# Value products in blocks of four key tiles from the first head on, and half of the later query projections ahead of the attention

## The chip, the cores and the metric

The kernel runs on one core of a Trainium2 chip. The metric is the device time of one execution in microseconds; for several executions the median is given.

## The reference

Two branches share the input `x` (2048 x 512, float32) and are mixed by a gate per row: multi-query attention with 32 heads of 16 columns and one key and one value head, and a gated feed-forward layer with 1792 hidden columns.

```python
q = (x @ wq).reshape(B, S, H, Dh).transpose(0, 2, 1, 3)      # S = 2048, H = 32, Dh = 16
k, v = x @ wk, x @ wv                                        # one head, shared by all 32
p = softmax(einsum("bhqd,bkd->bhqk", q, k) * Dh ** -0.5)
a = einsum("bhqk,bkd->bhqd", p, v).transpose(0, 2, 1, 3).reshape(B, S, H * Dh) @ wo
b = (silu(x @ w_gate) * (x @ w_up)) @ w_down
g = sigmoid((x * gate_w).sum(-1, keepdims=True))
out = g * a + (1 - g) * b
```

## The kernel before

**Arithmetic.** Every projection is done in three matmuls, since each operand is split into a high and a low part of a reduced float32 format: high by high, high by low, low by high (`three`). A job of the class `Job` is one 128 x 512 result in a PSUM buffer "pf" (there are three), made of 12 or 15 such matmuls, its *steps*. When its last step is issued, its `end` empties the buffer.

**Stages.** First `x` is transposed in four chunks of 512 columns, and keys and values are projected. Then come the queries. The query weights are cut into four column groups `m` of eight heads each; `query(m, c)` is the job for group `m` and chunk `c`. Group 0 (the first eight heads) is done at once. The other groups' twelve jobs stand at the head of the list `JOBS`, followed by the feed-forward jobs: gate and up per hidden tile, and down. `fill(GAP)` runs the first 36 steps of the list, three query jobs, as whole 128-row matmuls before the attention begins.

**The attention.** A unit `u` is one head and one of its 16 key tiles. `score(u, j)` makes two matmuls on the two 64-row halves of the array, into one of two PSUM buffers "pss" (1024 columns); `exps` lets ACT write the exponentials into a tile "pt". `mix(u)` multiplies a whole "pt" with the value tile, in four matmuls of 32 columns, and adds into "po". Between scores, `feed(k)` issues `k` steps of jobs: in the attention a job's steps are halved by rows, and `Halves` pairs the low half of one job with the high half of another (each feed issues at most two 64-row matmuls). What order all this has is written out by hand under a manual schedule.

For the first two heads a loop of `BEGIN = 16` rounds does two key tiles each: four scores and eight feeds, then two `mix`. From unit 32 on, `block(k, ...)` does four key tiles: 8 scores and 16 feeds in the order of `STEPS`, then four `mix`. In a block some scores are read half by ACT and half by DVE (letter H in `KINDS`: DVE copies 512 columns out of PSUM and ACT does their exponential later). The first block of all, k = 8, has an order of its own (`TURN`), because it must score ten tiles ahead where others score eight. "pt" comes from the pools `bp` and, from the release of the query pool on, a second pool of the same size.

**Where queries go.** The end of a query job, `keep`, makes three parts: `qh` and `ql`, and `qb`, the absolute value times the largest key norm, of which a running maximum `top` decides at the end whether a safe path must be run. Group 0 uses two passes of ACT and three tiles of the rings "hh" and "hl", seven tiles each; other groups use four passes of DVE, one tile of each ring and one of "hs" or "ht" (two each). DVE's maximum comes last. The three parts go to `q_d` in DRAM by three DMAs (`store`) from the queue of SP, which issues in order; heads of later groups are read back by `load_head`. Stores of group 0 are collected in `STORES` and issued before the last group's weights are loaded. A ring hands a tile out again only when all that read it is done, DMAs included.

**After the attention.** Jobs that are left run as whole matmuls, while the last head's sums are inverted and stored; then `finish` multiplies the attention's output with `wo`, and adds the feed-forward part.

## Time and profile before

| | |
|---|---|
| median of 3 runs | 1343.92 us (1343.49 to 1346.85) |
| the profiled execution | 1344.01 us, its span 1341.9 us |
| busy: PE, ACT, DVE, POOL | 1328.0, 1061.6, 722.4, 391.0 us |
| DMA | 107.79 MB, mean 80 GB/s |
| first score, first value product | 47.93 us, 53.37 us from the span's start |
| first block of four, its value product | 137.35 us |
| last value product ends, output projection begins | 1262.7 us, 1290.2 us |

The busy time of PE counts pipelined matmuls, whose ends are modelled. In rows of the timeline the columns are the start and the length in us, engine, line, operation, what is written and read, the shape and the number; a bracket gives the idle time ahead of it and what ended it. SPq rows are DMA issues on the queue of SP.

### The profile page before, as it was taken

The page shows a single profiled execution, that of the slowest core. Times are in us where ns is not written, and L with a number is a line of the kernel's source. Part 1 is how long each engine was busy: PE and PEld are TensorE (multiplying, and loading weights), DVE is VectorE, ACT ScalarE, POOL GpSimd, SP SyncE. Part 2 cuts the span into 40 slices and gives each one's busy share as a digit, 9 for nine tenths or more (in the row PEclk, how much of TensorE's full clock was granted, in tenths as well). Part 3 has the DMA queues.
Part 4 walks back from the last instruction along what each step waited for, and adds up shares of the span by engine and source line. Part 5 has one row for each costly group of instructions (what it writes and reads, how often), then busy time and mean ns, then how long its engine had stood idle before and what let it go on. Part 6 is the DMA issues. An engine that isn't in the chain of part 4 may idle for free. (4 is left out here: it accounts for less than half of the span.)

```text
span 1341.9 us, 26802 instructions
## 1 busy us (share of the span) xinstructions
PE 1328.0 (99%) x10743; PEld 770.4 (57%) x10743; DVE 722.4 (54%) x1221; ACT 1061.6 (79%) x1463; POOL 391.0 (29%) x408
## 2 busy tenths in 40 slices
PE   9999999999999999999999999999999999999997
PEld 7655555555555555555555555555555555555576
DVE  5554565555455555555464555455454565465432
ACT  4578888888888888888888888888888888888400
POOL 6140321152042151152131241142131241333343
PEclk9999999999999999999999999999999999999999
DMA  8455221131122221141131221231121221222154
GB/s 277 142 173 190 65 60 38 35 107 44 44 86 77 78 80 38 35 107 44 52 122 39 82 79 39 57 83 45 52 61 30 81 79 39 74 68 60 44 161 143
DMA packets 101489, 107.79 MB, mean 80 GB/s; under 512 B 9968, under 2 KB 69616, under 8 KB 99696
## 3 DMA queue, kind: packets, MB, share of 16 engines
q1 hardware_dynamic: 99632, 105.81, 27.5%
q8 instruction: 88, 1.44, 0.5%
q10 hardware_dynamic: 1728, 0.20, 0.1%
q14 instruction: 41, 0.34, 0.1%
HBM read 76.09 MB, written 29.36 MB: 79 GB/s over the span
## 5 line engine op out<-in xcount | busy, mean ns | idle before, releaser
L668 ACT ACTIVATE pt<-pss 128x1024 f32<-128x1024 f32 (+1 forms) x1024 | 842.0, 876 | 177.3 <-PE pss L660 146.3
L664 DVE COPY pt<-pss 128x512 f32<-128x512 f32 x354 | 244.8, 692 | 415.6 <-PE pss L660 380.6
L680 PE MATMUL po<-pt,vaug 128*32 128x512 f32 x4096 | 467.6, 595 | 0.0
L660 PE MATMUL pss<-qs,ks 64*128 64x512 f32 x2048 | 403.1, 417 | 1.1 <-ACT pt L668 1.1
L660 PEld LDWEIGHTS pss<-qs,ks 64*128 64x128 f32 x2048 | 193.7, 184 | 218.4 <-ACT pt L668 183.6
L680 PEld LDWEIGHTS po<-pt,vaug 128*32 128x32 f32 x4096 | 119.2, 109 | 260.2 <-issue 255.2
L668 ACT ACTIVATE pt<-pt 128x512 f32<-128x512 f32 x354 | 195.7, 620 | 0.0
L176 PE MATMUL pf<-xh,wgl 64*128 64x512 f32 (+1 forms) x440 | 162.0, 392 | 0.0
L176 PE MATMUL pf<-xh,wgh 64*128 64x512 f32 (+1 forms) x440 | 160.5, 391 | 0.5 <-DVE acc L331 0.2
L176 PE MATMUL pf<-xl,wgh 64*128 64x512 f32 (+1 forms) x440 | 160.2, 390 | 0.0
L176 PE MATMUL pf<-xh,wuh 64*128 64x512 f32 (+1 forms) x440 | 158.4, 391 | 0.7 <-DVE sign L403 0.3
L176 PE MATMUL pf<-xl,wuh 64*128 64x512 f32 (+1 forms) x440 | 158.2, 390 | 0.0
L176 PE MATMUL pf<-xh,wul 64*128 64x512 f32 (+1 forms) x440 | 157.3, 391 | 0.0
L106 POOL CAST wgh<-wraw 128x512 fp32r<-128x512 f32 x56 | 36.1, 644 | 402.6 <-PE pf L176 311.8
L176 PE MATMUL pf<-wdh,hh 64*128 64x512 f32 (+1 forms) x427 | 143.4, 391 | 1.7 <-DVE hh L106 1.7
L176 PE MATMUL pf<-wdh,hl 64*128 64x512 f32 (+1 forms) x427 | 144.1, 390 | 0.0
L176 PE MATMUL pf<-wdl,hh 64*128 64x512 f32 (+1 forms) x427 | 143.4, 390 | 0.0
L689 DVE RECIPROCAL rsb<-rsb 128x128 f32<-128x128 f32 x128 | 117.1, 935 | 10.1 <-issue 8.2
L106 POOL CAST wuh<-wraw 128x512 fp32r<-128x512 f32 x56 | 35.1, 626 | 298.2 <-PE pf L176 245.3
L176 PEld LDWEIGHTS pf<-xh,wgh 64*128 64x128 f32 (+1 forms) x440 | 78.5, 185 | 9.8 <-issue 2.5
L176 PEld LDWEIGHTS pf<-xh,wuh 64*128 64x128 f32 (+1 forms) x440 | 77.3, 185 | 9.3 <-issue 3.7
L176 PEld LDWEIGHTS pf<-xl,wgh 64*128 64x128 f32 (+1 forms) x440 | 78.5, 185 | 6.0
(157 smaller groups left out, 1547.6 us busy)
## 6 DMA issues: line engine op xcount, KB each, us to landing
wraw<-in_B_w_gate_dram SPq DMA_DIRECT2D x56, 256.0 KB
wraw<-in_B_w_up_dram SPq DMA_DIRECT2D x56, 256.0 KB
wraw<-in_B_w_down_dram SPq DMA_DIRECT2D x56, 256.0 KB
qs<-q_d SPq DMA_DIRECT2D x62, 192.0 KB
q_d<-hl SPq DMA_DIRECT2D x18, 256.0 KB
q_d<-hh SPq DMA_DIRECT2D x18, 256.0 KB
o_d<-osb SPq DMA_DIRECT2D x128, 32.0 KB
a_d<-acc SPq DMA_DIRECT2D x4, 1024.0 KB
```

The lines of the kernel that those rows point to most:

```text
L106: eng_hi.tensor_copy(hi, src)
L176: ins = nc.tensor.matmul(self.ps, a, b, start=(i == 0 and not half), stop=(last and half != 0))
L660: nc.tensor.matmul(ps[:, b * CH:(b + 1) * CH], ks[rows, kt * P:(kt + 1) * P], QS[h][rows, j, :], start=True, stop=True)
L664: other = nc.vector.tensor_copy(pt[:, CH:], ps[:, CH:]) if half else None
L668: ins = nc.scalar.activation(pt[:, w], ps[:, w], AF.Exp, scale=SCALE)
L680: nc.tensor.matmul(po[c * 2 * DH:(c + 1) * 2 * DH, :], vaug[:, kt, :], pt[:, c * CH:(c + 1) * CH], start=(kt == 0), stop=(kt == NT - 1))
L689: nc.vector.reciprocal(rsb[:, w], rsb[:, w])
```

## The change

`BEGIN`, `TURN` and their loop go: after an opening of four scores and eight feeds (`OPEN`) all 128 blocks are of four key tiles. For that all six "pt" buffers come from one pool (`PTB = 6`), and its space is had by freeing the query pool ahead of the attention: `qpool` now holds only the chunks 2 and 3 of `x`, and the query weights lie in `wqpool` of their own. The list of query jobs is ordered by chunk (2, 3, then 0, 1) instead of by group, and `GAP` is 72: the six jobs of chunks 2 and 3 run before the attention, as whole matmuls, and are emptied as group 0 is, by ACT with three tiles of the two rings. The six others run in the attention and are emptied by DVE; the scaling, the absolute value with the store, and the maximum are put on the list `DEFER` and run between blocks. `load_wq(3)` is issued before the stores of group 0. The maximum over `top` moves behind the attention.

```diff
-GAP = 36
+GAP = 72
-PTB = 3
+PTB = 6
-BEGIN = 16
-TURN = "SS" + "SFF" * 8
+OPEN = "SFSFFFSFFFSF"
...
+    wqpool = tc.alloc_tile_pool(name="wqpool", bufs=1, side="right")
...
-        WQ[m] = load_split(wq_v[:, :, m * P:(m + 1) * P], f"wq{m}", 1, qpool)
+        WQ[m] = load_split(wq_v[:, :, m * P:(m + 1) * P], f"wq{m}", 1, wqpool)
...
-            if m:
-                qb = wp.tile([P, CH], F32, name="ht" if c % 2 else "hs", bufs=2)
+            behind = m and c in ORDER[:2]
+            if behind:
+                qb = wp.tile([P, CH], F32, name="ht" if (m + c) % 2 else "hs", bufs=2)
                 nc.vector.tensor_copy(qh, ps)
             else:
                 qb = wp.tile([P, CH], F32R, name="hl" if c % 2 else "hh", bufs=7).bitcast(F32)
                 nc.scalar.activation(qh, ps, AF.Copy)
                 nc.scalar.activation(qb.bitcast(F32R), ps, AF.Abs, scale=kmax)
...
+            if behind:
+                DEFER.extend([((m, c), 0.5, scale), ((m, c), 0.7, bound), ((m, c), 0.7, most)])
             else:
-                STORES.append(store)
-            nc.vector.tensor_reduce(top[:, t:t + 1], qb, axis=AX.X, op=ALU.max)
+                if m:
+                    store()
+                else:
+                    STORES.append(store)
+                most()
...
-        jobs = [query(m, c) for m in range(1, KD) for c in range(NCH)]
+        jobs = [query(m, c) for c in ORDER[2:] + ORDER[:2] for m in range(1, KD)]
...
+            load_wq(3)
             run(STORES, NCH)
-            load_wq(3)
             fill(GAP)
+    qpool.release()
...
-            for n in range(BEGIN):
...
-            for k in range(2 * BEGIN // BLOCK, NB):
+            tiles = [(u, j) for u in range(2) for j in range(2)]
+            for what in OPEN:
+                if what == "S":
+                    exps(*score(*tiles.pop(0)))
+                else:
+                    feed(1)
+            for k in range(NB):
                 u = BLOCK * k
-                if k == 2 * BEGIN // BLOCK:
-                    n = u + 6 - (u + 1)
-                    block(k, u + 1, u + 6, TURN, "A" * 2 * n, [f"{i}d" for i in range(2 * n)])
-                elif k == NB - 1:
+                if k == NB - 1:
...
+        nc.vector.tensor_reduce(top[:, KD * NCH:], top[:, :KD * NCH], axis=AX.X, op=ALU.max)
...
-            if len(JOBS) == TC:
+            if len(JOBS) <= TC and OUTS[1] not in OT:
                 load_o(OUTS[1])
```

What this makes of the instructions is seen at three places. The first is PE, in the first head. Before, around the second pair of value products (L660 is a score, L680 a value product, each "pt" one key tile):

```order
L660 MATMUL pss_782<-qs_257,ks_78 128x512 x2
L680 MATMUL po_742<-pt_731,vaug_79 32x512 x4
L680 MATMUL po_742<-pt_751,vaug_79 32x512 x4
L660 MATMUL pss_795<-qs_257,ks_78 128x512 x2
L660 MATMUL pss_799<-qs_257,ks_78 128x512 x2
```

And now, around the first value products (a score is L669, a value product L689):

```order
L669 MATMUL pss_853<-qs_260,ks_78 128x512 x2
L669 MATMUL pss_856<-qs_260,ks_78 128x512 x2
L689 MATMUL po_861<-pt_766,vaug_79 32x512 x4
L689 MATMUL po_861<-pt_780,vaug_79 32x512 x4
L689 MATMUL po_861<-pt_793,vaug_79 32x512 x4
L689 MATMUL po_861<-pt_810,vaug_79 32x512 x4
L669 MATMUL pss_879<-qs_260,ks_78 128x512 x2
```

Where two key tiles stood between scores, four stand.

The second is ACT, where the projections give way to the attention. Before (L217 and L218 empty a query job of group 0, L668 is an exponential):

```order
L217 ACTIVATE hh_501<-pf_488 128x512
L218 ACTIVATE hh_503<-pf_488,kmax_83 128x512
L217 ACTIVATE hh_525<-pf_512 128x512
L218 ACTIVATE hl_527<-pf_512,kmax_83 128x512
L668 ACTIVATE pt_696<-pss_697 128x1024
L668 ACTIVATE pt_696<-pss_701 128x1024
```

And now (L218 and L219 are the copy and the absolute value, L677 an exponential; the last five of the six early jobs):

```order
L218 ACTIVATE hh_593<-pf_580 128x512
L219 ACTIVATE hh_595<-pf_580,kmax_83 128x512
L218 ACTIVATE hh_616<-pf_603 128x512
L219 ACTIVATE hh_618<-pf_603,kmax_83 128x512
L218 ACTIVATE hh_639<-pf_626 128x512
L219 ACTIVATE hl_641<-pf_626,kmax_83 128x512
L218 ACTIVATE hh_662<-pf_649 128x512
L219 ACTIVATE hl_664<-pf_649,kmax_83 128x512
L218 ACTIVATE hh_685<-pf_672 128x512
L219 ACTIVATE hl_687<-pf_672,kmax_83 128x512
L677 ACTIVATE pt_766<-pss_767 128x1024
L677 ACTIVATE pt_766<-pss_773 128x1024
```

Twelve passes of ACT, two for each early job, now stand between the last pass of group 0 and the first exponential.

The third is the queue of SP. Before, at the end of the stores of group 0 (L232 is a store to `q_d`, L137 a load of weights):

```order
L232 DMA q_d_69<-hl_526 8x16x512
L232 DMA q_d_69<-hh_525 8x16x512
L232 DMA q_d_69<-hl_527 8x16x512
L137 DMA wraw_548<-in_A_wq_dram 128x4x128
L232 DMA q_d_69<-hl_568 8x16x512
L232 DMA q_d_69<-hh_567 8x16x512
L232 DMA q_d_69<-hs_569 8x16x512
```

And now (a store is L230):

```order
L230 DMA q_d_69<-hl_529 8x16x512
L230 DMA q_d_69<-hh_528 8x16x512
L230 DMA q_d_69<-hl_530 8x16x512
L230 DMA q_d_69<-hl_571 8x16x512
L230 DMA q_d_69<-hh_570 8x16x512
L230 DMA q_d_69<-hh_572 8x16x512
L230 DMA q_d_69<-hl_594 8x16x512
```

The load of the weights has gone from between the stores to their head, and the early jobs' parts follow group 0 directly, 18 stores of them before the next head's queries are read, where there were nine.

More of the change, by code (lines that the diff above doesn't have):

```diff
@@ L219, in keep @@
             nc.vector.tensor_tensor(ql, ps, qh.bitcast(F32), ALU.subtract)
-            if m:
-                nc.vector.tensor_scalar(qb, qh.bitcast(F32), kmax, None, op0=ALU.mult)
-                nc.vector.scalar_tensor_tensor(qb.bitcast(F32R), qb, -1.0, qb, op0=ALU.mult, op1=ALU.max)
             parts = [ql, qh, qb.bitcast(F32R)]
@@ L629, in tile_gated_mix @@
                     nc.vector.tensor_scalar(c_sb, g_sb, -0.5, 0.5, op0=ALU.mult, op1=ALU.add)
+            load_wq(3)
             run(STORES, NCH)
-            load_wq(3)
             fill(GAP)
+            assert not DEFER
+    qpool.release()
+    for c in ORDER[2:]:
+        XC.pop(c)
     PO, LATER = [], []
@@ L646, in load_head @@
                 nc.sync.dma_start(qs[b * RT + DH:(b + 1) * RT], qv[b])
-        def new_pt(u):
-            late = u > PTB * (BEGIN * 2 // PTB) and (u - 2 * BEGIN) % (2 * PTB) >= PTB
-            PT[u] = (PAIR[1] if late else bp).tile([P, S], F32, name="pt", bufs=PTB)
         def score(u, j, half=False):
@@ L655, in score @@
             if j == 0:
-                new_pt(u)
+                PT[u] = bp.tile([P, S], F32, name="pt", bufs=PTB)
             ps = ps_s.tile([P, 2 * CH], F32, name="pss")
@@ L815, in tile_gated_mix @@
             print("steps", halves.steps, "idle", halves.idle, "left", len(JOBS))
-    PAIR.pop().release()
     with tc.tile_pool(name="tpool", bufs=2) as tp, tc.tile_pool(name="rpool", bufs=1, side="right") as rp, \
```

37 lines of the change are left out of this document (8 added, 29 removed).

## The prediction

> **What bounds the kernel now.** I read the page first: which engine fills the span, and how far the others are from it.
>
> ```profile
> span 1341.9 us, 26802 instructions
> PE 1328.0 (99%) x10743; PEld 770.4 (57%) x10743; DVE 722.4 (54%) x1221; ACT 1061.6 (79%) x1463; POOL 391.0 (29%) x408
> ```
>
> PE is busy for 1328.0 of 1341.9 us, so the time is the length of PE's instruction stream plus its holes. The change therefore has to be priced as steps of PE, as the price of regrouping them, and as holes that it opens or closes. The table by stretches (columns: stretch, its length, then busy us of PE, PEld, DVE, ACT, POOL, granted clock, share of the DMA engines, GB/s) shows the four stretches that the change touches:
>
> ```profile
> 53.37:126.50 73.13, 73.13 (x601) 38.86 (x600) 38.41 (x70) 56.86 (x61) 19.91 (x20) 1.00 0.57 187
> 128.36:137.35 8.99, 8.04 (x56) 4.18 (x52) 3.81 (x8) 8.45 (x11) 0.00 (x0) 1.00 0.71 190
> 137.35:203.26 65.91, 65.91 (x562) 36.85 (x560) 38.27 (x66) 55.74 (x79) 21.52 (x22) 1.00 0.19 52
> 1262.72:1290.20 27.48, 25.82 (x116) 20.79 (x112) 17.04 (x22) 1.26 (x2) 19.05 (x21) 1.00 0.38 100
> ```
>
> They are the first two heads with products of two key tiles, the block that turns to groups of four (PE idle there for 0.95 us), the first blocks of four, and the jobs left over after the attention. PE's timeline gives the period of each:
>
> ```profile
> 43.76 0.39 PE L176 MATMUL pf<-xh,wq1h 128*128 128x512 f32 x1
> ...
> 47.61 0.39 PE L176 MATMUL pf<-xh,wq1l 128*128 128x512 f32 x1
> 47.93 0.73 PE L660 MATMUL pss<-qs,ks 64*128 64x512 f32 x4
> ...
> 53.37 1.92 PE L680 MATMUL po<-pt,vaug 128*32 128x512 f32 x16
> ...
> 126.50 1.92 PE L680 MATMUL po<-pt,vaug 128*32 128x512 f32 x16
> 128.36 0.73 PE L660 MATMUL pss<-qs,ks 64*128 64x512 f32 x4
> 130.03 0.50 PE L660 MATMUL pss<-qs,ks 64*128 64x512 f32 x2 [0.95 <-ACT pt L668]
> ...
> 137.35 3.64 PE L680 MATMUL po<-pt,vaug 128*32 128x512 f32 x32
> 140.92 0.73 PE L660 MATMUL pss<-qs,ks 64*128 64x512 f32 x4
> ...
> 203.26 3.64 PE L680 MATMUL po<-pt,vaug 128*32 128x512 f32 x32
> ```
>
> From 53.37 to 126.50 are 15 periods: 4.875 us for two key tiles, 9.75 for four. From 137.35 to 203.26 are 7: 9.416 us for four, with the same 8 scores and 16 feeds. A product of four takes 3.57 us (137.35 to 140.92), so one of the 24 score or feed slots takes (9.416 - 3.57) / 24 = 0.244 us. A whole-array step of a job takes (47.61 - 43.76) / 17 = 0.2265 us.
>
> **The PE stream without waits.** PE's work is the same in kind and nearly in number. Thirty-six steps (three query jobs) move ahead of the attention: its first score moves from 47.93 to 47.93 + 36 x 0.2265 = 56.1. What follows is paced by the exponentials at first:
>
> ```profile
> 48.62 3.77 ACT L668 ACTIVATE pt<-pss 128x1024 f32<-128x1024 f32 x4 [7.57 <-issue]
> ```
>
> The first starts 0.7 us after the first score and four take 3.77. There are two score buffers, so the sixth score needs the fourth exponential's end, 56.1 + 0.7 + 3.8 = 60.6; it and the 22 slots left of the opening and of block 0 take 23 x 0.244 = 5.6, and the first product comes at 66.2. Eight blocks later, at 66.2 + 8 x 9.416 = 141.5, stands the product that stood at 137.35: 4.1 us later. In return the tail holds 6 jobs instead of 9, by the order of PE 72 steps of 128x512 instead of 111: 39 x 0.2265 = 8.8 us less. The net is 4.1 - 8.8 = -4.7 us. The turning block with its hole is in that: it is gone.
>
> Edits that I take at nothing, with the rows for their covers (DVE's five passes of one query job, one score copy, and the hole in the tail):
>
> ```profile
> 42.60 0.69 DVE L214 CAST hh<-pf 128x512 fp32r<-128x512 f32 x1 [0.22 <-PE pf L176]
> 43.32 0.69 DVE L219 TENSOR_TENSOR hl<-pf,hh 128x512 fp32r<-128x512 f32 x1
> 43.93 0.48 DVE L221 TENSOR_SCALAR hs<-hh,kmax 128x512 f32<-128x512 f32 x1
> 44.45 0.69 DVE L222 SCALAR_TENSOR_TENSOR hs<-hs 128x512 fp32r<-128x512 f32 x1
> 45.17 0.69 DVE L238 TENSOR_REDUCE top<-hs 128x1 f32<-128x512 f32 x1
> L664 DVE COPY pt<-pss 128x512 f32<-128x512 f32 x354 | 244.8, 692 | 415.6 <-PE pss L660 380.6
> 1281.03 0.47 PE L176 MATMUL pf<-wdh,hh 128*128 128x512 f32 x1 [1.66 <-DVE hh L106]
> ```
>
> The last maximum, now on DVE after the attention, lies under a job of PE there. The remaining six query jobs cost DVE 1.3 jobs a block, each with these five passes (3.24 us), 4.3 us, beside three score copies of 0.69: 6.4 of 9.4 us, so DVE keeps up; if it did not, scores would wait, by at most a pass (0.7) per block, 3 us in five blocks. The shorter tail covers the last head's division, store and reload less: PE waited there 1.66 us in the stretch already, and I bound the difference at 0 to 1 us, taking nothing.
>
> **The wait that comes in.** Each early job now leaves by ACT (copy and absolute value) instead of DVE, and takes three tiles from the rings "hh" and "hl" of seven each, where it took two and one from "hs" or "ht". The four projections of the first heads hold six of each, and a tile comes free only when its store to q_d has landed. The trace has one such wait, and these rows of SP, DVE and POOL price it:
>
> ```profile
> 43.63 0.77 SPq L232 DMA_DIRECT2D q_d<-hl  x1
> 44.45 1.29 SPq L232 DMA_DIRECT2D q_d<-hh  x2
> ...
> 56.37 1.26 SPq L232 DMA_DIRECT2D q_d<-hl  x1
> 57.73 1.13 SPq L137 DMA_DIRECT2D wraw<-in_A_wq_dram  x1
> 58.96 1.32 SPq L232 DMA_DIRECT2D q_d<-hl  x1
> 60.33 0.60 SPq L232 DMA_DIRECT2D q_d<-hh  x1
> 61.06 1.08 SPq L232 DMA_DIRECT2D q_d<-hs  x1
> 49.42 0.69 DVE L214 CAST hh<-pf 128x512 fp32r<-128x512 f32 x1 [3.57 <-DMA q_d<-hh]
> 64.39 0.61 POOL L106 CAST wq3h<-wraw 128x512 fp32r<-128x512 f32 x1 [27.61 <-DMA wraw<-in_A_wq_dram]
> ```
>
> The stores leave SP about 1.3 us apart, and the stretch has the DMA engines half free (share 0.57 in the first row of the table), so it is the stores' own pace. The second store, issued at 44.45, frees its tile at 49.42: 5.0 us. The load issued at 57.73, behind a full queue, has landed at 64.39: 6.7 us. In the changed kernel a job asks for three stores (3.9 us) where its matmuls take 12 x 0.2265 = 2.7 us, so DMA paces this stretch. The six jobs' ACT passes reuse, in order, the tiles of stores 2; 3 and 5; 8 and 9; 11 and 7; 14 and 10; 15 and 13 (stores 1 to 12 are the first projections', 13 to 15 the first job's own). ACT is in order, and all twelve passes stand ahead of the first exponential. So the exponentials start when store 15 has landed and the last job's two passes are done:
>
> ```profile
> 37.16 0.60 ACT L217 ACTIVATE hh<-pf 128x512 fp32r<-128x512 f32 x1 [1.54 <-PE pf L176]
> 37.65 0.68 ACT L218 ACTIVATE hh<-pf,kmax 128x512 fp32r<-128x512 f32 x1
> ```
>
> Store 15 has in front of it what the store issued at 61.06 had: twelve stores, one load (now first instead of thirteenth), two stores. It lands between 61.06 + 5.0 = 66.1 and 61.06 + 6.7 = 67.8; I take 67.8, since the load's row lies in the same full queue. The two passes take 1.2 us (37.16 to 38.33), the first exponential starts at 69.0 instead of 56.8, and everything behind it is 12.2 us late (10.5 at the early bound). PE meanwhile is held at the start of the fourth, fifth and sixth job, each wanting one of three "pf" buffers that a held ACT has not read, and at last at the third score, which wants the first exponential. The load of wq3 moves ahead of the stores on SP; its job may start 2 to 4 us late, which lies inside the same wait.
>
> One more price hangs on this. PE's last hole there lasts from about 65 (the sixth job can start when store 9 has landed and been passed, about 61, and runs 2.7 us, then five slots) to 70, some 4 to 6 us. At the kernel's end the rows show what such a hole does to the clock (columns PE busy, clock, DMA share, GB/s):
>
> ```profile
> 1335.82 0.39 PE L116 MATMUL pf<-wo3h,xl 128*128 128x512 f32 x1
> 1336.00:1339.00 3.00, 0.20 (x1) 1.00 0.31 96
> 1339.00:1342.00 3.00, 0.00 (x0) 0.57 0.03 8
> ```
>
> The last matmul ends at 1336.2 and the mean clock of the last 3 us is 0.57: if it falls to half, it fell near 1339.4, 3.2 us after. If the clock stays at half as long as it took to fall, 3.2 us of work take 1.6 longer; between nothing and that I take 0.8, since the exponentials pace half of that stretch. [...]
>
> Sum against the profiled execution (1344.01 us, its span 1341.9 and 2.1 around it; the median of the runs is 1343.92, so nothing is to be corrected): 1344.0 - 4.7 + 12.2 + 0.8 = 1352.3 us.
>
> **The rivals.**
> 1. Forecast: ACT waits for stores ahead of the attention, **1352.3 us**. For it: the row at 49.42, where the eighth "hh" waited 3.57 us for the second store. Its own range is 1349.5 (early landing, no fall of the clock) to 1355 (the fall in full, and a pass or two of DVE in the way). Chance 0.65.
> 2. The stores do not hold ACT, because they land faster once no attention runs beside them. Then the regrouping is left: 1344.0 - 4.7 = **1339.3 us**, faster. It decides at the first exponential: up to 56.8 + 4.7 = 61.5 it is a gain, for which fifteen stores would have to land by 60.3, 1.1 us apart from 44 on rather than 1.3 and 6 us behind. For it: PE had no hole from 53.37 to 126.50. Against: from 43.63 to 56.37 eleven stores left SP 1.16 us apart, the first three faster than the rest, with only queries and scores beside them. Chance 0.13.
> 3. A partial hold: tiles come free earlier than counted, since the rings hand out whichever is free, and the wait is 4 to 8 us: **1340 to 1348 us**. The order's own waits name the stores listed above, which speaks against it. Chance 0.10.
> 4. The hold, and the weights of the gate and up projections late as well. They and the next head's queries stand on SP behind 30 stores instead of 21, 9 x 1.3 = 12 us later. The second head's scores start some 25 us after the opening and the first gate job some 45, so there is cover; if a chain of late stores (a "hs" or "ht" tile not free) stops DVE for 3 to 5 us in blocks 4 to 6, it is **1355 to 1358 us**. Chance 0.12.
>
> **How the numbers follow.** About 0.3%, 4.0 us, is what a measurement of this kernel can tell from no change: 1340 to 1348 counts as the same. Faster is rival 2 (0.13), the same rival 3 (0.10), slower the forecast and rival 4 (0.77). The predicted time is the forecast's. The range leaves out rival 2 and the lower half of rival 3 below, and the end of rival 4 above: 1345 to 1357 us.
>
> **What would show it.** Right: in ACT's rows of the changed kernel the copies of the third to sixth job each wait for a DMA on q_d, the first exponential stands near 69 us instead of 48.6, PE shows holes between 45 and 70 us that sum to about 13, and products of four from the first head on come every 9.4 us; the eighth period later stands near 154. In the tail 39 steps, 8.8 us, are gone. The step on the clock is right if the granted clock is below 1.00 near 70 us. Wrong: a first exponential before 61.5 us (rival 2 or 3), periods above 9.6 us in blocks 0 to 7 (then DVE is in the way), or a tail that is less than 8 us shorter (then the last head's division is exposed).

## The result, and the profile after

The changed kernel takes 1366.2 us, the median of six runs (1362.2 to 1367.7), beside 1345.4 for the kernel before on the same chip: a ratio of 1.0152 with a 95% interval of 1.0134 to 1.0170. It is slower by 20.9 us, where the prediction had 8.3. The direction and the wait for stores hold; the size does not.

The profiled execution is the fastest of the six: 1362.21 us with a span of 1360.4, against 1344.01 and 1341.9 before. The two traces therefore differ by 18.5 us. The median of the changed kernel lies 4.0 us above its profiled execution (mean clock 0.989 to 0.991 in the other runs instead of 0.992), that of the kernel before 1.4 above its own.

The predicted wait is there. These are ScalarE's rows (start, duration, line, operation, and in brackets the idle time ahead of it with what ended it):

```profile
52.10 0.69 ACT L219 ACTIVATE hh<-pf,kmax 128x512 fp32r<-128x512 f32 x1 [7.27 <-DMA q_d<-hh]
...
67.80 0.60 ACT L218 ACTIVATE hh<-pf 128x512 fp32r<-128x512 f32 x1 [2.70 <-DMA q_d<-hh]
...
70.17 2.85 ACT L677 ACTIVATE pt<-pss 128x1024 f32<-128x1024 f32 x3
```

The copies of the second to the fifth early job each wait for a store to q_d, by ScalarE's rows. The sixth has only 0.14 us left to wait once the fifth is done, but the chain of work that ended last runs through its store, the fifteenth (start, duration, what):

```profile
62.95 6.05 DMA q_d<-hh
...
69.11 0.60 ACT hh L218
```

This is the store that the prediction had named. The first exponential starts at 70.2 us; the prediction had 69.0. What TensorE waited for in the whole span (us in total, times, longest):

```profile
PE pf L176 <- DVE hl L220: 3.1, 2, 2.1
PE pss L669 <- ACT pt L677: 2.8, 3, 2.5
...
PE pf L176 <- POOL wq3h L106: 1.6, 1, 1.6
```

The first two and the last are the holes of the opening, 7.5 us together, where the prediction had about 13. The first names VectorE because the "pf" buffer is read by ScalarE's copy and then by VectorE's subtraction, which waits for that copy. The same stretch by windows (stretch, its length, PE busy and count, granted clock, share of the DMA engines, GB/s) shows what the prediction gave 0.8 us:

```profile
58.00:62.00 4.00, 2.71 (x12) 1.00 0.53 204
62.00:66.00 4.00, 3.19 (x8) 0.61 0.53 204
...
71.00:74.00 3.00, 2.46 (x12) 0.85 0.52 200
74.00:77.00 3.00, 3.00 (x10) 0.50 0.53 204
77.00:80.00 3.00, 3.00 (x13) 0.51 0.55 206
80.00:83.00 3.00, 3.00 (x26) 1.00 0.53 203
```

The clock falls to half three times, the first time ahead of these rows, behind the wait of 1.6 us for wq3 (0.56 between 50 and 53 us). From the windows' mean clocks I estimate 3.4, 3.4 and 6.8 us at half speed. The first two falls stretch the early jobs by some 3.4 us, which takes the place of holes; the wait for stores hides them almost whole (the first exponential stands at 69.1 us in x_warm_tail below, which has neither of the two, its steps taking 0.39 or 0.40 us from 49.9 to 64.3 us, and at 68.9 in x_tail, which has both, with steps of 0.63 from 49.4 and from 62.3 us). The third lies on the path. The products that mark the stages, the first of the kernel, the first of the ninth period and the first of the last period, stand here; behind them the two rows of the kernel before:

```profile
82.23 1.07 PE L689 MATMUL po<-pt,vaug 128*32 128x512 f32 x8
...
158.97 1.50 PE L689 MATMUL po<-pt,vaug 128*32 128x512 f32 x12
...
1283.21 2.35 PE L689 MATMUL po<-pt,vaug 128*32 128x512 f32 x20
```

```profile
137.35 1.06 PE L680 MATMUL po<-pt,vaug 128*32 128x512 f32 x8
...
1259.14 1.06 PE L680 MATMUL po<-pt,vaug 128*32 128x512 f32 x8
```

| stage, us | before | predicted | after | more than predicted, by this stage alone |
|---|---|---|---|---|
| first exponential | 48.6 | 69.0 | 70.2 | 1.2 |
| first product | 53.4 | 79.2 | 82.2 | 1.8 |
| ninth period | 137.4 | 154.5 | 159.0 | 1.5 |
| last period | 1259.1 | 1276.2 | 1283.2 | 2.5 |
| end of the span | 1341.9 | 1350.2 | 1360.4 | 3.2 |

The prediction's entries are its sum, stage by stage: its first product at 66.2 plus 12.2 and 0.8, and the ninth period and all later ones at the time of before plus 4.1 + 12.2 + 0.8. No stage is far off; each is late by 1 to 3 us, and all in the same direction. The start-up, whose code did not change, is alone 1.6 us late in this execution (the first copy of a query job starts at 32.52 us, at 30.88 before), so that the first exponential would have been 0.4 us early without it.

The last row is the tail, from the last period to the end: 82.8 us before, 77.2 after, 5.6 less and not 8.8. Under 8 was one of the prediction's signs of being wrong. SyncE's queue there (start, duration until the last of the group is issued), after and before:

```profile
1301.32 11.23 SPq L438 DMA_DIRECT2D wraw<-o_d  x5
1312.60 0.42 SPq L346 DMA_DIRECT2D a_d<-acc  x1
1313.13 0.38 SPq L824 DMA_DIRECT2D again<-a_d  x1
...
1317.28 1.05 SPq L438 DMA_DIRECT2D wraw<-o_d  x2
```

```profile
1291.18 0.33 SPq L337 DMA_DIRECT2D a_d<-acc  x1
1291.60 0.38 SPq L837 DMA_DIRECT2D again<-a_d  x1
...
1302.49 8.02 SPq L429 DMA_DIRECT2D wraw<-o_d  x4
```

Before, the last accumulator's store and the first one's reload, 1 MB each, left 11 us ahead of the loads for the third output chunk. After, with three jobs fewer, they leave 4 us ahead of them, and the longest of the waits for that chunk is this one:

```profile
1330.51 0.50 PE L116 MATMUL pf<-wo2h,xh 128*128 128x512 f32 x1 [1.23 <-POOL xh L106]
```

### The profile page after: what moved, and what is told of

It reads as the page before. It is cut to its first block, busy times and chain, and to the rows that moved or that the text cites. A ratio compares the mean times of both kernels' runs of the same rounds, so it can differ in the third digit from the quotient of the medians.

```text
span 1360.4 us, 26895 instructions
## 1 busy us (share of the span) xinstructions
PE 1337.0 (98%) x10746; PEld 780.3 (57%) x10746; DVE 724.4 (53%) x1230; ACT 1072.2 (79%) x1502; POOL 389.5 (29%) x408
## 4 chain that ended last, share of the span: by engine, by line
PE 90%; DMA 4%; DVE 2%; ACT 1%; POOL 1%; SPq 1%; issue 1%; DVEq 0%; POOLq 0%; ACTq 0%
PE pf L176 34%; PE po L689 33%; PE pss L669 19%; PE pf L116 2%; DMA wraw<-o_d 2%; ACT pt L677 1%; DMA q_d<-hh 1%; SPq L230 1%; DMA wraw<-in_B_w_down_dram 1%; POOL xl L107 1%; PE pss L551 0%; DVE rsb L698 0%; PE po L538 0%; DMA wraw<-in_B_w_gate_dram 0%; DVE pt L673 0%
## 5 line engine op out<-in xcount | busy, mean ns | idle before, releaser
L677 ACT ACTIVATE pt<-pss 128x1024 f32<-128x1024 f32 (+1 forms) x1024 | 832.3, 864 | 167.6 <-PE pss L669 142.7
L673 DVE COPY pt<-pss 128x512 f32<-128x512 f32 x381 | 263.5, 692 | 436.9 <-PE pss L669 395.3
L689 PE MATMUL po<-pt,vaug 128*32 128x512 f32 x4096 | 466.0, 595 | 0.0
L669 PE MATMUL pss<-qs,ks 64*128 64x512 f32 x2048 | 404.7, 417 | 3.2 <-ACT pt L677 2.8
L669 PEld LDWEIGHTS pss<-qs,ks 64*128 64x128 f32 x2048 | 196.4, 184 | 213.4 <-ACT pt L677 174.7
L689 PEld LDWEIGHTS po<-pt,vaug 128*32 128x32 f32 x4096 | 120.2, 110 | 263.1 <-issue 257.5
L677 ACT ACTIVATE pt<-pt 128x512 f32<-128x512 f32 x381 | 210.6, 620 | 0.0
L176 PEld LDWEIGHTS pf<-xh,wgh 64*128 64x128 f32 (+1 forms) x444 | 78.2, 185 | 10.9 <-issue 3.0
L176 PEld LDWEIGHTS pf<-xh,wgl 64*128 64x128 f32 (+1 forms) x444 | 78.3, 185 | 6.3 <-POOL wgl L107 0.6
```

The lines of the kernel that those rows point to most:

```text
L176: ins = nc.tensor.matmul(self.ps, a, b, start=(i == 0 and not half), stop=(last and half != 0))
L669: nc.tensor.matmul(ps[:, b * CH:(b + 1) * CH], ks[rows, kt * P:(kt + 1) * P], QS[h][rows, j, :], start=True, stop=True)
L673: other = nc.vector.tensor_copy(pt[:, CH:], ps[:, CH:]) if half else None
L677: ins = nc.scalar.activation(pt[:, w], ps[:, w], AF.Exp, scale=SCALE)
L689: nc.tensor.matmul(po[c * 2 * DH:(c + 1) * 2 * DH, :], vaug[:, kt, :], pt[:, c * CH:(c + 1) * CH], start=(kt == 0), stop=(kt == NT - 1))
```

## The experiments

Four theories were put to the test; the last has no experiment of its own. **Stores**: the backlog of scratch stores holds ScalarE, and with it the attention. **Clock**: TensorE's waits of about 2 us also halve its clock, and part of that lies on the path. **Tail**: the two 1 MB transfers collide with the third chunk's loads. **Blocks**: the blocks of four from the first head on cost something of their own. Every kernel was timed beside the kernel before on the same chip, whose medians were 1345.4 to 1347.0.

| kernel | what differs from the changed kernel | us | ratio to before, 95% interval |
|---|---|---|---|
| changed | | 1366.2 | 1.0152 [1.0134, 1.0170] |
| x_early_alone | loop and pools of before | 1366.4 | 1.0138 [1.0118, 1.0158] |
| x_tail | tail transfers moved | 1360.0 | 1.0102 [1.0087, 1.0118] |
| x_warm | 118 dummy products | 1365.2 | 1.0131 [1.0112, 1.0150] |
| x_warm_tail | x_tail, 146 dummy products | 1358.5 | 1.0095 [1.0080, 1.0111] |
| x_rows16 | scratch rows spread | 1369.0 | 1.0174 [1.0160, 1.0189] |
| x_rows16_split | same, reads split | 1363.7 | 1.0136 [1.0118, 1.0154] |
| x_soon | six stores issued sooner | 1366.0 | 1.0156 [1.0137, 1.0174] |
| x_best | same, tail, last weights early | 1362.1 | 1.0127 [1.0108, 1.0146] |
| x_free | spread, split, three stores sooner, weights, tail | 1357.9 | 1.0085 [1.0072, 1.0098] |
| x_free_warm | same, dummy products | 1354.9 | 1.0063 [1.0050, 1.0075] |
| x_act | nine stores from ScalarE's queue, tail | 1356.5 | 1.0071 [1.0059, 1.0083] |
| x_act2 | same, last weights earlier | 1358.0 | 1.0073 [1.0057, 1.0089] |
| x_act3 | same, spread, split | 1348.1 | 1.0014 [1.0005, 1.0024] |
| x_act4 | as x_act3, four reads a head | 1353.1 | 1.0055 [1.0043, 1.0067] |
| x_tail_before | kernel before, tail transfers moved | 1346.5 | 1.0001 [0.9991, 1.0012] |

### Which half of the change costs

x_early_alone is the kernel before with the early jobs, their evacuation and the order of the loads:

```diff
-GAP = 36
+GAP = 72
...
-        jobs = [query(m, c) for m in range(1, KD) for c in range(NCH)]
+        jobs = [query(m, c) for c in ORDER[2:] + ORDER[:2] for m in range(1, KD)]
...
-            if m:
+            behind = m and c in ORDER[:2]
+            if behind:
...
+            load_wq(3)
             run(STORES, NCH)
-            load_wq(3)
             fill(GAP)
```

> The kernel before with only the early half of the change: six query jobs ahead of the attention, in the order of chunks, two of their three evacuating operations on ScalarE, and the last weights loaded first; loop, pools and the old opening of sixteen blocks of two stay. If the early half costs all that is lost and the blocks of four gain the 4 us that the sum had for them: 1368 to 1373, with the first exponential near 70 us. Rival (the blocks of four cost too, through VectorE's order in the first eight blocks): under 1364.

1366.4 us, between the two expectations: the early half alone costs as much as the whole change. Its first product stands at 71.5, 18.1 us later than before, and then it is caught a second time, since all steps of a query job still stand together on VectorE. VectorE's row and TensorE's:

```profile
124.33 0.48 DVE L222 TENSOR_SCALAR ht<-hh,kmax 128x512 f32<-128x512 f32 x1 [7.77 <-DMA q_d<-ht]
127.40 0.79 PE L176 MATMUL pf<-xh,wuh 64*128 64x512 f32 x1 [3.47 <-DVE sign L404]
```

So the loss begins in the early half, and what the blocks of four give or cost cannot be read from this kernel's time alone. The other half, blocks of four without the early jobs, was not run.

### The tail

```diff
     def store_acc(c, now=False):
+        if c == ORDER[-1] and not now:
+            return
         nc.sync.dma_start(a_d[c], ACC[c])
...
         ACC[0] = rp.tile([P, TC, D], F32, name="again")
+        nc.sync.dma_start(ACC[0], a_d[0])
...
-        nc.sync.dma_start(ACC[0], a_d[0])
         for m, c in enumerate(OUTS):
...
+            if m == 1:
+                store_acc(ORDER[-1], True)
```

> The changed kernel with two 1 MB transfers of the tail moved: the accumulator of the first chunk is read back ahead of the last query jobs' loads, and that of the last chunk is stored behind the loads for the last output chunk. Theory 3 (with fewer jobs left, these two transfers fall on the loads for the third output chunk and leave TensorE waiting): its waits near 1328.8, 1330.5, 1331.9 and 1332.6 us, 2.7 us together, go, and the time falls by 2 to 4 us, to 1362 to 1364. Rival (the tail is bound by GpSimd's splits of what is loaded, not by when it lands): unchanged within 1 us, 1365 to 1367.

> The kernel before with the same two 1 MB transfers of the tail moved. Theory 3 (the collision comes from the change, since with nine jobs left the transfers passed ahead of the loads): unchanged, 1343.5 to 1347. Rival (the two transfers cost in either kernel): 1339 to 1342.

The changed kernel gains more than expected, 1366.2 to 1360.0; the kernel before gains nothing (1.0001). The collision is the change's own. In the profiled executions the tail is 73.4 us instead of 77.2, the 8.8 less that the prediction had plus 0.6. The windows in which TensorE works on the third chunk, in the changed kernel and then in x_tail, show that its waits cost twice, once themselves and once by the clock:

```profile
1330.00:1334.00 4.00, 2.47 (x6) 0.83 0.96 326
1334.00:1338.00 4.00, 4.00 (x13) 0.74 0.39 122
```

```profile
1330.00:1334.00 4.00, 3.39 (x15) 1.00 0.86 288
1334.00:1338.00 4.00, 4.00 (x20) 1.00 0.25 76
```

3.8 of the 6.2 us are seen in these two traces. The rest lies in runs that were not profiled, and what it is was not shown.

### The clock

Small products of a constant, which nobody reads, fill TensorE's waits without shortening them:

```diff
+DUMMY = {2: 26, 4: 14, 5: 34}
...
         while left[0] > 0 and JOBS:
             left[0] -= JOBS[0].size
+            for _ in range(DUMMY.get(made, 0)):
+                nc.tensor.matmul(pw[:, :P], warm2, warm2, start=True, stop=True)
...
-            for what in OPEN:
+            for i, what in enumerate(OPEN):
+                for _ in range({6: 38, 10: 6}.get(i, 0)):
+                    nc.tensor.matmul(pw[:, :P], warm2, warm2, start=True, stop=True)
```

> The changed kernel with 118 small products of a constant, which nobody reads, in TensorE's queue where its idle time lay: 26, 14 and 34 ahead of the third, fifth and sixth early query job and 38 and 6 ahead of the third and fourth score. The waits themselves stay. Theory 2 (idle time of about 2 us lets the clock fall to a half for some 3.5 us, and from 71 us on that lies on the path): granted clock 1.00 from 48 to 80 us, first exponential still at 69 to 71 us, first product of values at 78 to 79 instead of 82.2 us, 1366.2 falls by 2 to 6 us, to 1360 to 1364. Rival (the clock falls for other reasons, or its loss is hidden behind the stores): 1365 to 1368, or later where the small products outlast the waits.

1365.2 us: not told apart from no change. The 38 products ran as soon as their turn came and ended early, and behind the rest of the wait, 1.57 us, the clock fell (TensorE's row, and the window behind it):

```profile
66.02 2.29 PE L792 MATMUL po<-ident 128*128 128x128 bf16 x38
69.89 0.50 PE L676 MATMUL pss<-qs,ks 64*128 64x512 f32 x2 [1.57 <-ACT pt L684]
74.00:78.00 4.00, 4.00 (x13) 0.50 0.53 204
```

x_warm_tail has 66 products there instead of 38, on top of x_tail.

> The kernel with the two transfers of the tail moved (1360.0 us), with the small constant products added again, now 66 instead of 38 ahead of the third score, so that they last through the wait there (each took 0.060 us, and 1.57 us were left uncovered). The waits stay. Theory 2 (a wait of about 1.5 us ahead of 70 us halves the clock for up to 10 us on the path): granted clock 1.00 from 60 to 85 us, first exponential still at 68.5 to 70 us, first product of values 3 to 5 us sooner than 83.2, and 1360.0 falls to 1355 to 1357. Rival (the clock falls there for another reason): clock 0.50 again behind 70 us, 1359 to 1362.

The profiled executions of x_tail and x_warm_tail show what one wait costs. First exponential and first product of x_tail:

```profile
68.85 2.94 ACT L679 ACTIVATE pt<-pss 128x1024 f32<-128x1024 f32 x3
83.25 1.06 PE L691 MATMUL po<-pt,vaug 128*32 128x512 f32 x8
```

and of x_warm_tail, with the window behind the wait:

```profile
69.12 2.85 ACT L686 ACTIVATE pt<-pss 128x1024 f32<-128x1024 f32 x3
70.00:74.00 4.00, 3.22 (x22) 1.00 0.53 198
78.94 1.49 PE L698 MATMUL po<-pt,vaug 128*32 128x512 f32 x12
```

From the first exponential to the first product it is 14.4 us with the clock at half and 9.8 with the clock held: 4.6 us for one wait. The time fell by only 1.5 us, less than expected and within the two intervals, so the price is shown by these two traces and not by the times. The profiled span fell by 2.5; the tail was 1.8 us longer there (75.2), and why was not followed. The same repair on x_free is told below.

### The stores

First the stores were made shorter. One store had eight heads outermost; now it has 128 rows, and a head is read back in eight pieces instead of four:

```diff
-    q_d = dpool.tile([H, 3 * DH, S], F32, name="q_d")
+    q_d = dpool.tile([3, H * DH, S], F32, name="q_d")
...
-                    nc.sync.dma_start(q_d[m * HG:(m + 1) * HG, j * DH:(j + 1) * DH, cs], part.bitcast(F32))
+                    nc.sync.dma_start(q_d[j, m * P:(m + 1) * P, cs], part.bitcast(F32))
...
+                for i, part in enumerate((1, 0, 1, 2)):
+                    nc.sync.dma_start(qs[b * RT + i * DH:b * RT + (i + 1) * DH], qv[part, b])
```

> The changed kernel with the scratch copy of the queries laid out as three blocks of 512 rows, so that one store has 128 rows outermost instead of eight heads. Theory 1 (the stores' pace holds ScalarE's copies): a 256 KB store passes in about half of the 1.3 us that it takes now, store 15 lands near 58 instead of 67.8 us, the first exponential starts at 59 to 62 us instead of 70.2, TensorE's idle time of 0.98, 2.11 and 2.47 us ahead of 57.69, 62.81 and 71.25 us goes, and with it the clock's fall behind it: 1366.2 falls by 8 to 11 us for the wait and by 2 to 5 us for the clock, to 1350 to 1356. Rival (the copies wait for something else than the stores' pace, TensorE's banks or the bytes moved): first exponential at 69 to 71 us, 1364 to 1368.

> The kernel with the rows of the scratch copy spread (1369.0 us), with the eight reads for the next head issued as four in each of two blocks instead of eight in one. If the reads' issue (5.0 us on SyncE, ahead of a gate weight that TensorE then waited 2.5 us for, with the clock's half speed behind it) is what ate the gain of the shorter stores: the step of 4.9 us near block 105 goes, the first exponential stays at 64 to 66 us, and the time falls to 1362 to 1365. Rival (the reads cost wherever they stand): 1367 to 1370.

Here x_rows16 missed its number, 1369.0. The first exponential moved the way that was expected, though not all of it: it starts at 64.81 us instead of 70.17, where 59 to 62 was expected. Much later, the eight reads took the gain back. SyncE's queue and TensorE in the 106th block:

```profile
1075.61 5.01 SPq L659 DMA_DIRECT2D qs<-q_d  x8
1080.72 0.53 SPq L137 DMA_DIRECT2D wraw<-in_B_w_gate_dram  x1
1085.39 0.50 PE L176 MATMUL pf<-xh,wgh 64*128 64x512 f32 x1 [2.52 <-POOL wgh L106]
```

The gate weight stands behind 5.0 us of issuing, TensorE waits for it, and the clock falls again behind that wait (steps of 0.62 us from 1087.27 us on, where others take 0.39). With the reads split over two blocks the step is gone and the time is 1363.7, as expected.

The other way is to issue stores sooner, while the DMA engines have little to do (a share of 0.18 to 0.23 between 36 and 44 us in the changed kernel).

```diff
                     job.step(i)
+                if c in (1, 2):
+                    run(STORES, 1)
                 if c == 0:
```

> The changed kernel with one thing moved: the scratch stores of the first two chunks of query group 0 (six of the thirty) are issued as soon as the next chunk's copies have been, near 38 and 42 us, where the DMA engines stand at a share of about 0.2, instead of behind all four, near 46 us. Theory 1 (the stores' backlog holds ScalarE's copies): store 6 and all behind it land some 8 us sooner, the first exponential starts at 60 to 63 us instead of 69 to 70, TensorE's idle time ahead of the last early jobs is under 1 us each and that ahead of the third score is gone; with the clock (theory 2) 1366.2 falls by 10 to 13 us, to 1353 to 1356; without theory 2 by 7 to 9, to 1357 to 1359. Rival (SyncE is late with head 0's query copies instead, or the loss lies elsewhere): first exponential behind 65 us, 1362 to 1368.

1366.0 us, no gain: the rival. SyncE's issues follow one another, 0.53 to 0.67 us each from 50.80 us on here, and six stores between the sixteen copies of head 0 push the load of the last weights back, from 45.30 to 52.10 us. SyncE's row, and TensorE's wait for those weights:

```profile
52.10 0.53 SPq L137 DMA_DIRECT2D wraw<-in_A_wq_dram  x1
55.89 0.80 PE L176 MATMUL pf<-xh,wq3h 128*128 128x512 f32 x1 [9.46 <-POOL wq3h L106]
```

x_best adds the tail's repair and loads those weights right behind the third group's.

> The changed kernel with three repairs: six stores issued sooner, the two transfers of the tail moved, and the last query weights loaded right behind the third group's. If the wait for stores (9 to 12), the clock behind it (3.4), the wait for the last weights (1.6, partly hidden) and the tail's collision with its clock (4 to 6) make up the loss, 1366.2 falls to 1343 to 1350. If more is lost in the blocks themselves, 1351 to 1356.

1362.1 us, missed: the load left SyncE only at 35.1 us, the copies behind it started 3 us later than in x_soon, and the first exponential stood at 70.5 again.

x_free combines the spread rows, the split reads, the tail's repair, and only the first chunk's three stores and the last weights moved forward.

> The changed kernel with the backlog taken away as far as I can: rows of the scratch copy spread, reads split over two blocks, the stores of the first chunk issued and the last query weights loaded behind the second chunk's copies, and the tail's two transfers moved. If the wait for stores is 12 us of the loss as predicted and the clock and the tail the rest: first exponential at 58 to 62 us, TensorE idle for under 2 us in all between 45 and 75 us, clock 1.00 there, and 1360.0 falls by 6 to 11 us (the spread reads cost 2.5), to 1349 to 1354. Rival (what holds the attention back is not the stores): first exponential behind 65 us, 1357 to 1362.

> The kernel with the backlog reduced (1357.9 us) with the small constant products in the waits that are left there: 6 and 22 ahead of the fifth and sixth early job (0.33 and 1.40 us), 66 and 6 ahead of the third and fourth score (3.83 us). Theory 2 (in that kernel 13.65 us at half clock, 6.8 us lost, follow the wait of 3.83 us and eat the gain of the shorter backlog): clock 1.00 from 45 to 85 us, first product of values 4 to 6 us sooner than 78.2, the time falls to 1351 to 1354. Rival (the clock falls for another reason than the wait): clock again 0.50 behind 66 us, 1356 to 1359.

x_free starts its exponentials at 63.9, 4.9 us ahead of x_tail, but gains only 2.1, and its 1357.9 us is the rival's time. Its windows tell where the rest went, and those of x_free_warm that it comes back:

```profile
66.00:70.00 4.00, 3.73 (x12) 0.50 1.01 373
...
74.00:78.00 4.00, 4.00 (x22) 0.55 0.39 112
```

```profile
66.00:70.00 4.00, 3.63 (x38) 1.00 1.01 334
70.00:74.00 4.00, 3.34 (x20) 1.00 0.94 339
```

A wait of 3.83 us ahead of the third score is followed by more than 10 us at half clock; with the dummy products the clock is 1.00 there, and 1357.9 becomes 1354.9, a little above what was expected (the two intervals overlap at their ends). The first product came 1.9 us sooner and not 4 to 6, because in that execution the first exponential itself stood 2.6 us later (66.5).

Last, ScalarE's own queue issues the nine stores of the first three chunks, from 32 us on:

```diff
-            def store():
+            def store(eng=nc.sync):
...
+                if c == 1:
+                    load_wq(3)
+                if c < 3:
+                    STORES.pop(0)(nc.scalar)
```

The order of the three stores of a job changes with it.

> The changed kernel with the layout of the scratch copy as it was, but the nine stores of the first three chunks of query group 0 issued from ScalarE's own queue as each chunk is evacuated, from about 33 us on, while the DMA engines stand at a share of 0.2; the last query weights loaded behind the second chunk's copies, and the tail's two transfers moved. At 1.3 us each, store 12 should then land near 50 instead of 64 us and no ring be full when an early job needs it. If the backlog of the stores and the clock behind the waits are the loss: first exponential at 57 to 60 us, no wait of TensorE over 1 us between 45 and 75 us, clock 1.00, and 1360.0 falls by 11 to 15 us, to 1345 to 1349, the kernel before's time within 0.3%. Rival (ScalarE, with issues of 0.5 to 0.8 us each between its copies, falls behind and hands its delay to TensorE): first exponential behind 63 us, 1354 to 1360.

> The kernel with nine stores issued from ScalarE's queue (1356.5 us) with the load of the last query weights moved forward by one chunk, ahead of the second chunk's head 0 copies: there it was issued at 44.84 us and TensorE waited 6.90 us for it, at 53.04. If the backlog of the stores is the loss: that wait is under 1 us, the first exponential starts at 59 to 63 instead of 68.0 us, and 1356.5 falls by 5 to 9 us, to 1347 to 1351. Rival (SyncE's and ScalarE's issues, up to 5.2 us for three while the other queue's stores are under way, set the pace whatever is stored when): first exponential behind 65 us, 1354 to 1358.

> The same with the rows of the scratch copy spread and the reads split over two blocks, so that each store takes about 0.9 instead of 1.3 us. If the backlog is the loss: first exponential at 58 to 61 us, no wait of TensorE over 1 us between 45 and 70 us, clock 1.00, and with the 2.5 us that the spread reads cost 1347 to 1351. Rival (issues set the pace): first exponential behind 63 us, 1353 to 1357.

TensorE in x_act again waited 6.90 us for the last weights. x_act2 is without that wait, but its first exponential still stands at 67.7: with stores on both queues a group of three copies took SyncE 5.2 us to issue in x_act (1.8 and 2.2 in the changed kernel), and in x_act2 its own stores began at 55.7 us. Both missed. In x_act3 the stores are short as well (eleven in a row leave SyncE 0.61 us apart, from 46.28 to 53.00 us), and no early job waits for one any more (ScalarE waits once, 2.8 us at 42.4 us, ahead of them). Its first exponential, the one wait of TensorE over 0.5 us between 36 and 84 us, the window in which x_free had its half clock, and the three products that mark the stages:

```profile
57.91 2.85 ACT L681 ACTIVATE pt<-pss 128x1024 f32<-128x1024 f32 x3
58.99 0.50 PE L673 MATMUL pss<-qs,ks 64*128 64x512 f32 x2 [0.64 <-ACT pt L681]
66.00:70.00 4.00, 4.00 (x40) 1.00 0.70 163
67.27 1.06 PE L693 MATMUL po<-pt,vaug 128*32 128x512 f32 x8
...
144.32 1.06 PE L693 MATMUL po<-pt,vaug 128*32 128x512 f32 x8
...
1273.06 1.50 PE L693 MATMUL po<-pt,vaug 128*32 128x512 f32 x12
```

1348.1 us, 11.9 under x_tail. The first product stands 16.0 us ahead of x_tail's: 10.9 from the first exponential, which is the wait for stores, and 5.0 from there to the product, which is the clock. Between the ninth product and the last it loses 4.5 us against the changed kernel (1128.7 against 1124.2). All of that is in the third of each four periods, the one behind the reads of the next head. But 1.9 of it is a single period of 11.25 us, where the clock is down behind a wait of 1.8 us for VectorE (the product of values from 279.14 us on takes 4.8 us instead of 3.6); the other 29 take 9.49 us in the mean instead of 9.40.

> The kernel at 1348.1 us (spread rows, nine stores from ScalarE's queue, early last weights, tail transfers moved) with each head read back in four transfers as in the kernel before, two of them with three blocks of sixteen rows, instead of eight of sixteen rows. Its loop from the ninth product to the last took 1128.7 us, against 1124.2 in the changed kernel, and the third of each four periods 9.55 instead of 9.40 us, the one in which the next head's first scores stand. If the eight reads are the cause (a first score waits for eight transfers): that period is 9.40 again and 1348.1 falls by 3 to 5 us, to 1343 to 1345, under the kernel before. Rival (the start of the next head costs whatever the number of reads, or three outer rows make the reads slow and the weights behind them late): 1347 to 1353.

Missed: 1353.1. Yet the period that the expectation is about did come down: its median is 9.45 us instead of 9.52, with 9.42 in the changed kernel. So most of what these periods lose goes with the eight reads. What was not foreseen is one place. In the 106th block a gate weight, which left SyncE behind the four reads of a head, two of them with three blocks outermost, came late, and TensorE waited 5.0 us for it:

```profile
1077.06 0.79 PE L176 MATMUL pf<-xh,wgh 64*128 64x512 f32 x1 [4.99 <-POOL wgh L106]
```

With the half clock behind that wait (steps of 0.62 us from 1077.65 us on, where others take 0.39) this one period takes 16.37 us, 7.0 more than its neighbours, which is more than the whole loss against x_act3. In the changed kernel the same load also follows four reads, in their old form, and landed 3.8 us after its issue; TensorE waited 0.2 us for it. That the new form of the reads holds the load up is the likely cause, and no further run isolates it. So no version beat the kernel before; x_act3 comes within 0.14%.

## Why the prediction was right, and where not

What failed are three terms of the sum that were put too low: the tail's shorter cover and VectorE's part, both taken at nothing, and the clock, taken at 0.8 us. The term that the prediction was built on, the wait for stores, held.

**The wait for stores: right, and its size nearly so.** It had the first exponential at 69.0 with the wait and 56.8 without, 12.2 us. The chip has 70.2 with it and, in x_act3, 57.9 without it. That these also differ by 12.3 is luck, since the start-up was 1.6 us late in the one execution and 0.6 in the other; with that taken off the wait is 11.2 us, and 11.4 if x_tail is set against x_act3. The fifteenth store, taken to land at 67.8 us, landed at 69.0; the late start-up is more than that difference. Where nothing else took their place on SyncE, shorter or earlier stores moved the exponential (64.8 us in x_rows16, 63.9 in x_free, 57.9 in x_act3). Rival 2 needed it before 61.5 us in the changed kernel and rival 3, with a wait of up to 8 us, before 64.8; both fall.

**The clock, taken at 0.8 us: mis-sized.** The step is "if the clock stays at half as long as it took to fall, 3.2 us of work take 1.6 longer", with half of that hidden; that it stays down that long was the author's estimate, and no row of before shows the return. It missed twice. The fall needs no wait of 3.2 us: it came behind 1.57 us of idleness in x_warm and behind 1.6, 2.1 and 2.5 us in the changed kernel, though not behind 1.4 us in the same trace (at 291.5 us, clock 1.00 on both sides) nor behind 1.66 us in the kernel before (at 1281.0 us, clock 1.00 from 1276 to 1292 us). What decides it was not shown. And the half speed can last longer: 3.4 us for the two falls in front of the first exponential, as long as was assumed, but 6.8 for the one behind it, 10.2 in x_warm and 13.6 to 13.7 in x_free and x_tail (my estimates from the windows' mean clocks). Why it lasts so differently is open. On the path one such wait costs 4.6 to 5.0 us (x_warm_tail and x_act3 against x_tail); in the profiled execution of the changed kernel, the fastest of the six, 2.7 (12.1 from exponential to product, against 9.4 in x_act3).

**The tail, whose shorter cover was taken at nothing (0 to 1 us): mis-sized, and by the runs the most.** The 39 steps are worth what was said, since without the collision the tail is 73.4 (x_tail) and 73.9 us (x_act3) instead of 82.8. So the last head's division, which the prediction would have blamed for a long tail, was not it. The prediction had looked only at that division and the reload, and not at what else SyncE has in order there. Fewer jobs moved two 1 MB transfers onto the third chunk's loads: 3.8 us by the traces, 6.2 by the medians, the clock's part included.

**"DVE keeps up", taken at nothing, bound 3 us: too kind.** Blocks 0 to 7 took 76.7 us instead of 8 x 9.416 = 75.3 here, and 77.1 in x_act3, where no store holds ScalarE in front of them. Both have two periods of 9.9 to 10.0 us, above the 9.6 that the prediction named as a sign. In each of them, in the changed kernel, a score starts 0.14 us after a score copy of VectorE that stands behind two passes of a query job (the copy ends at 127.81 us, the score starts at 127.95). The sum of 6.4 of 9.4 us was not the question, but the order in which VectorE does it. The later periods took 1124.2 instead of 1121.8 us, of which one wait for VectorE in the 22nd block is 1.4; the rest of the 3.9 us that all these blocks lose was not traced. Taken from the regrouping's -4.7, this leaves a net gain near 0.8 us, and rival 2's 1339.3 was probably not to be had even without the wait.

**What is left.** In the profiled execution the late start-up goes with a clock of 0.61 between 12 and 16 us; the kernel before had 1.00 there in its trace. The excess over the forecast, stage by stage, is 1.2 us at the first exponential (1.6 start-up, less 0.4), 1.8 clock, 1.5 and 2.5 blocks and 3.2 tail, which makes the 10.2 us between 1350.2 and 1360.4. The 4 us by which the median lies above this execution have their clock (0.989 to 0.991) as the only trace; x_tail takes more than its trace explains, so a part may be in the tail. That was not followed further. Why the reads of a head slow the period behind them stays open too.

Rival 4 did not happen in the changed kernel: no weight came late in blocks 4 to 6. It did happen, in its own way, in x_early_alone (VectorE held for 7.8 us by a store).

## What to carry to other kernels

Where work is moved ahead of a stage, count its transfers against their ring of buffers, their pace and the queue that issues them: here the transfers and not the matmuls set the start, to within about 1 us of the estimate. Then price a new wait of the matmul engine twice, once for itself and once for the clock behind it (here 4.6 to 5.0 us on the path behind one wait of 2.5), in the opening as in the tail. A repair that moves transfers has to be followed along its whole queue, since four of them here (x_rows16, x_soon, x_act, x_act4) handed the wait to a later load. And a mean over periods should be looked at one by one: single periods of 16.37 and 11.25 us look like a slow stage in it.

## What the hardware showed that was not expected

- A wait of 1.57 us (x_warm) was followed by the half clock (0.50 between 74 and 78 us), one of 1.66 us (the kernel before, at 1281.0 us) was not, and a wait of 3.83 us (x_free) by over 10 us of it (0.50 to 0.55 between 66 and 78 us), although TensorE was busy all through those 10 us (busy 3.73 to 4.00 in windows of 4).
- With eight heads outermost in a store the share of the DMA engines was 0.52 to 0.55 between 53 and 83 us (changed kernel); with 128 rows outermost it was 0.97 to 1.09 between 50 and 66 us (x_act3). The pace did not double with the share: between 58 and 62 us 271 GB/s moved in x_free at a share of 1.05 and 204 in the changed kernel at 0.53, and fifteen stores in a row left SyncE 0.68 us apart in x_free instead of 1.21 (from 46.32 to 56.51 us, and from 45.89 to 64.11 in the changed kernel).
- A second queue with stores on it went with slower issues on the first: with nine stores of eight heads outermost on ScalarE's queue, SyncE's issue of three 32 KB copies took 5.19 us and of single ones 1.06 to 1.66 (x_act, from 34.25 to 46.58 us), beside 1.84 and 2.19 for three and 0.51 to 0.58 for one in the changed kernel (from 34.44 to 45.21 us), which has no stores on a second queue; with 128 rows outermost single ones took 0.54 to 0.58 (x_act3, from 43.79 to 46.23 us).
